# Background steps held behind a matmul, statistics moved into a later pass: one change to a Trainium2 kernel

## The chip, the cores and the metric

The kernel runs on one core of a Trainium2 chip. The core has a matrix engine (TensorE, PE in the profile; PEld is its weight load), VectorE (DVE), ScalarE (ACT), GpSimd (POOL) and SyncE (SP). In this kernel every DMA is issued from SP's queue. Each engine takes its instructions in the order written into the program and waits at the head of its queue until what that instruction needs is there. The metric is the device time in microseconds (us) of one execution.

## The reference

Two blocks work on one layer-normed input x of 2048 tokens by 1024 features, in float32.

```python
xn = layernorm(x)
q, k, v = heads(xn @ wqkv)                      # 32 heads of 32
phi(p) = concat(softmax(p @ w_phi), softmax(-(p @ w_phi)))
kv = sum over tokens of phi(k)^T v ;  z = sum over tokens of phi(k)
s = (phi(q) kv / (phi(q) z + 1e-6)) @ wo
h = sigmoid(xn @ w_gate) * (xn @ w_up)          # 3584 wide
g = silu(h @ w_down)
out = x + s * g
```

## The kernel before, in words

**Products.** Every large product is split twice. Each float32 operand becomes a high part (cast to the matrix engine's float32r on ACT, line 133) and a low part (a subtraction on DVE, line 134): the *split*. A product is then three matmuls (`mm3`, lines 142 to 144). On top of that each product of 2x2 blocks is done with seven block products instead of eight, named B11, B21, T2, T3, T4, T1, B22; their operands are block sums and differences, which POOL, DVE or, for chunk 0, the opening makes.

**Order.** The 2048 tokens are two chunks of 1024. After a hand-ordered opening (layer norm of chunk 0 and its V projection), the loop over `ops` runs: the rest of chunk 0's projections (K, then Q); pass 0 of the gate and up products (B11, B21 for 14 tiles); chunk 1's projections V, K, Q; pass 1 (T2, T3, T4 for 14 tiles); pass 2 (T1, B22). The down projection, the attention and the output follow, without the plan described next. An op is four quarter units of 12 matmuls, one for each of four banks; after each unit the bank is emptied (*evicted*) by ACT or DVE and written again by the next op.

**The plan of background steps.** All else is cut into steps that `later(n, f)` puts n quarter units ahead; `tick()`, called after each unit, traces those due. The steps that matter here:
- *x statistics* (`x_stats`, line 588): a 512 KB load of a token tile of chunk 1 into a slot of the ring `xstat`, then `x_moments` (two bn_stats and a bn_aggr on DVE, lines 595 and 596); `x_scales` makes scale and shift from all eight, `x_rows` turns them with 16 transposes on PE (line 607) into rows in slots 24 and 25.
- *x tasks* (`x_task`, line 611): load a transposed tile of chunk 1 (line 614) and two blocks of chunk 0 (line 617), apply the rows on DVE (line 625), make the block sums on POOL and store them.
- *q steps*: load a block of Q, spread it (lines 462 to 466), exponentials (line 470), sums and reciprocals, store. *k steps* (`k_load`, `k_spread`, `k_rest`, `kv_products`): the same for K, then a product of phi(k) with V on PE (line 520), into banks 4 to 7. ACT copies V and phi(k) (lines 507 and 508) for it.
- *weight sums* of the gate and up weights (`glu_sums`, line 376: four loads, `w_sums` with four POOL instructions, lines 280 to 283, and stores), *wo sums* (`o_sums`), and *operand loads* (`fetch_operand`, line 246: two loads at line 252, into slots 43 and 44, each with a split two or three units later).

**Who may stand where.** A planner orders each engine's queue at compile time with a timing of its own. What is traced earlier has precedence, but what is ready earlier may go first. `tc.issue_after(ins)` keeps instructions that are traced inside it, and that run on the engine of `ins`, from going ahead of `ins` in that queue; it adds no wait. In `tick()` (line 155) that `ins` is `last_dve[0]`, the last split or eviction of DVE traced so far. `queue2` does the same on SP behind the last weight load or projection store.

**Evictions and seeds.** `proj_out` (line 418) empties a projection's bank: copies on ACT, adds on DVE (line 432), and a store to `qkv_d` (line 425). In pass 1 each bank starts a tile from a seed: `fetch` (line 1099) loads four blocks of partial sums (line 1105), `seed` (copy at line 1115) puts them into the banks on ACT after the tile before is evicted.

Of the kernel before, what the change touches and what calls it, by code (L numbers as in the profile page):

```python
# [10 lines left out]
F32 = mybir.dt.float32  # L11
# [13 lines left out]
CTT = CT // P  # L25
# [20 lines left out]
B11, T2, T3, B21, T1, T4, B22 = range(7)  # L46
# [3 lines left out]
def hedgehog_glu_kernel(  # L50
# [12 lines left out]
    nc = tc.nc  # L63
# [29 lines left out]
    def block(name, first, n, dtype):  # L93
        again = blocks.get(name, (None, 0))[1]
        t = sb.tile([P, n, 2, HB], dtype, name=f"{name}_{again}", tag=name, bufs=1)
        blocks[name] = t, again + 1
        for i in range(n):
            slots[first + i] = t[:, i]
            where[first + i] = name, i
        return t  # L100
# [19 lines left out]
    def halves(*ids):  # L120
        return [slots[i][:, a] for i in ids for a in range(2)]
# [13 lines left out]
        last_dve[:] = [i.ins]  # L135
        return i

    last_dve = []

    def mm3(o, a, b, first, last, **kw):  # L140

        nc.tensor.matmul(o, a[0], b[0], start=first, stop=False, **kw)  # L142
        nc.tensor.matmul(o, a[0], b[1], start=False, stop=False, **kw)  # L143
        nc.tensor.matmul(o, a[1], b[0], start=False, stop=last, **kw)  # L144

    def cut(ab, s):
        return ab[0][:, s], ab[1][:, s]
# [4 lines left out]
    def later(n, f, *a):  # L152
        plan.setdefault(clock[0] + n, []).append((f, a))

    def tick():

        clock[0] += 1
        for f, a in plan.pop(clock[0], []):
            with tc.issue_after(last_dve[0]):
                f(*a)  # L160

    side = deque()
# [420 lines left out]

    ln8 = sb.tile([P, 4, CTT], F32, name="ln8")
    ws8, mv8 = ln8[:, :3], ln8[:, 2:]
    xstat = Ring((50, 51))

    def x_stats(n):
        xt = x_load(CTT + n, xstat.next())
        later(2, x_moments, n, xt)  # L590

    def x_moments(n, xt):
        st = small.tile([P, 2, 2, 6], F32, name=f"bn{CTT + n}", tag="bn")
# [498 lines left out]
    def queue2(n, f, *a):  # L1092

        def go():
            with tc.issue_after(last_load[0]):
                f(*a)
        later(n, go)
# [68 lines left out]
    sums = deque((f, s) for f in range(NJ) for s in range(2))  # L1166

    def begin_projection(c):

        if c == 0:  # L1170
            for k in range(4):
                queue2(4 * (4 + 2 * k), o_sums, k, halves(52, 53))
            for n in range(CTT):
                later(8 + 4 * n, x_stats, n)
            later(44, x_scales)
            return
        for t in range(EARLY):
            k_steps(1 + 9 * t, 0, t)
        for n in range(WEARLY):
            queue2(14 + 42 * n // WEARLY, glu_sums, *sums.popleft(), halves(43, 44))  # L1180

    def begin_pass(p):

        if p == 0:
            for n, k in enumerate(4 * a + q for q in range(4) for a in range(2)):
                later(4 + 8 * n, x_task, k)
            for n in range(NJ):
                q_steps(4 + 7 * n, n // 2, n % 2)
        elif p == 1:
            at = 1  # L1190
            for t in range(EARLY, 2 * TT):
                k_steps(at, *divmod(t, TT))
                at += 6
                if t % TT == TT - 1:
                    k_end(at + 2, t // TT)
                    at += 14
            for n in range(len(sums)):
                queue2(3 + 6 * n, glu_sums, *sums.popleft(), halves(43, 44))
        else:
            for n in range(NJ):  # L1200
                queue2(6 + 7 * n, wd_sums, n, halves(43, 44))
            qf_raw.items, qf_e.items = halves(52), (53, 54)
            for n in range(2):
                q_steps(8 + 40 * n, 7, n)

    phase = 0
    for n, (kind, c, what, i) in enumerate(ops):
# [3 lines left out]
        if kind == "proj":  # L1211
            if n == 8 or (c and (what, i) == (PROJ[0], B11)):
                begin_projection(c)
            first_slot = (XO1 if c else XO)[i]
            xo = run(first_slot, 4)
            for u in range(4):
                if i in opening:
                    pbank[u] = pmm.next()
                us = slice(u * P, (u + 1) * P)
                for k in range(4):  # L1220
                    mm3(pbank[u], (xo[:, k, 0, us], xo[:, k, 1, us]), pair(ws[k]),
                        i in opening and k == 0, k == 3, skip_group_check=True)
                step()
                proj_out(c, what, i, u, pbank[u])
                if c and (what, i) == (Q, B22):
                    seed(0, u)
                if u < 3:
                    tick()
            flow["used"] += 4
            while prep():  # L1230
                pass
            if what == Q:
                if c == 0:
                    if i == T2:
                        load_outer(B11, 1)
                    if i == T4:
                        block("x6", 24, 4, F32)
                        for q in range(4):
                            later(1 + q, x_rows, q)
                if c:  # L1240
                    m = order.index(i)
                    if m < 6:
                        load_outer((T2, T2, T3, T3, T4, T4)[m], m % 2)
                    if i == T1:
                        phase = 1
                        fetch(0)
                    if i == B22:
                        block("x1", 4, 4, F32)
                        m1 = halves(4, 5, 6, 7)
            tick()  # L1250
            continue

        phase, f = c, what
        m = f * len(PASSES[phase]) + PASSES[phase].index(i)
        if m == 0:
            if phase == 0:
                step(1000)
                for b in (0, 2):
                    block(f"x{b}", 4 * b, 4, F32)
            begin_pass(phase)  # L1260
        if (phase, i) in ((1, T3), (2, T1)):
            fetch(f + 1)
        for b in range(4):
            s, th = divmod(b, 2)
# [25 lines left out]
                pass  # L1290

        if phase == 0:
            for o in {18: (B11,), 19: (B21,), 20: (T2,), 26: (T3, T4), 27: (T1, B22)}.get(m, ()):
                load_operand(XO1[o], xo_d[o])
            if m == 27:
                block("p", 36, 2, F32R)
                block("p2", 38, 1, F32R)
        elif phase == 1 and (f, i) == (NJ - 2, T4):
            load_outer(T1, 0)
        elif phase == 1 and f == NJ - 1:  # L1300
            if i == T2:
                load_outer(T1, 1)
                load_outer(B22, 0)
            elif i == T3:
                load_outer(B22, 1)
            else:
                for b in (3, 5):
                    block(f"x{b}", 4 * b, 4, F32)
                uvfree.extend(halves(45, 46, 47, 50, 12, 13, 14, 15, 20, 21, 22, 23))
                hs_r.items = halves(48, 49, 51)  # L1310
                phase = 2
                fetched.clear()
                fetch(0)
        elif phase == 2 and f == NJ - 2 and i == T1:
            wfree.extend(range(16, 20))
# [266 lines left out]
```

## Time and profile before

| | |
|---|---|
| median of 3 runs | 2398.32 us (2398.09 to 2399.51) |
| the profiled execution | 2396.47 us |
| its span, first to last instruction | 2394.7 us |
| PE busy | 2364.6 us |
| DVE / ACT / POOL busy | 1605.9 / 1052.3 / 960.7 us |
| DMA queue of SP | 658 MB, 78.5% of 16 DMA engines' time |
| granted TensorE clock | 0.997 |

The profile comes from one execution. Its rows name an engine, the line of the code, the operation and the tiles (out<-in, buffer numbers left out); in a timeline row the two first numbers are the start and the length in us, and a bracket at the end tells how long the engine stood idle before it and what released it. A row "A <- B: total, times, longest" is a wait of A for B. In the tables by stretch each engine has its busy time, with the number of its instructions in parentheses; then come the granted clock, the DMA engines' busy share and GB/s. Matmuls are pipelined, so their lengths overlap. The opening ends near 145 us, chunk 0's projections run to 281 us, pass 0 to 586, chunk 1's projections to 843, pass 1 to about 1310.

### The profile page before, as it was taken

What the parts mean: (1) busy time and instruction counts of PE and PEld (TensorE: products, weight loads), DVE (VectorE), ACT (ScalarE), POOL (GpSimd) and SP (SyncE); (2) the same over time, 40 slices, a digit from 0 to 9 for tenths busy, and PEclk for the clock granted to TensorE, in tenths of its full rate; (3) what the DMA queues carried; (4) which work ended last, traced back from release to release, by engine and by line L of the source; (5) the groups of instructions that cost most, each with busy time, mean ns of one, the idle gap of its engine ahead of it and who ended that gap; (6) DMA issues with size and microseconds to landing.
All of it is one profiled execution on the core that took longest, in us unless ns stands there. A gap on an engine that the chain in (4) does not pass through costs nothing.

```text
span 2394.7 us, 32086 instructions
## 1 busy us (share of the span) xinstructions
PE 2364.6 (99%) x10972; PEld 1969.3 (82%) x10972; DVE 1605.9 (67%) x2103; ACT 1052.3 (44%) x1601; POOL 960.7 (40%) x617
## 2 busy tenths in 40 slices
PE   9999999999999899999999999999999999999999
PEld 8887888888888678788888888888888888888887
DVE  8636755653787677676655544344889988877776
ACT  7333444454433356555556322223443334455553
POOL 1233144621245125553001387785333334423556
PEclk9999999999999999999999999999999999999999
DMA  8799998884788899998554999897666766876665
GB/s 292 266 306 363 367 326 315 318 297 156 257 308 308 281 329 327 341 334 293 178 193 167 356 357 362 314 326 287 221 211 230 240 216 215 281 271 234 199 205 182
DMA packets 293492, 660.29 MB, mean 276 GB/s; under 512 B 37328, under 2 KB 37584, under 8 KB 288720
## 3 DMA queue, kind: packets, MB, share of 16 engines
q1 hardware_dynamic: 293328, 658.24, 78.5%
q8 instruction: 86, 1.41, 0.2%
q14 instruction: 78, 0.64, 0.1%
HBM read 393.61 MB, written 264.50 MB: 275 GB/s over the span
## 4 chain that ended last, share of the span: by engine, by line
PE 84%; DMA 7%; DVE 3%; POOL 3%; ACT 1%; issue 1%; SPq 1%; POOLq 0%; DVEq 0%; ACTq 0%
PE bank L142 26%; PE bank L143 26%; PE bank L144 26%; DMA fb<-w_gu 2%; PE bank L790 1%; PE bank L766 1%; DMA wg_d<-fb 1%; PE bank L331 1%; DMA qkv_d<-fc 1%; PE bank L520 1%; POOL fb L281 1%; DMA fc<-wo 1%; POOL fb L280 1%; DVE w L134 1%; DMA fb<-xr_d 1%
## 5 line engine op out<-in xcount | busy, mean ns | idle before, releaser
L142 PE MATMUL bank<-x,w 128*128 128x512 f32 x2352 | 916.0, 390 | 4.7 <-ACT bank L1115 4.0
L143 PE MATMUL bank<-x,w 128*128 128x512 f32 x2352 | 916.1, 390 | 0.0
L144 PE MATMUL bank<-x,w 128*128 128x512 f32 x2352 | 915.0, 390 | 0.0
L134 DVE TENSOR_TENSOR w<-fa,w 128x512 fp32r<-128x512 f32 (+1 forms) x458 | 431.6, 947 | 384.3 <-ACT w L133 380.7
L133 ACT CAST w<-fa 128x512 fp32r<-128x512 f32 (+1 forms) x458 | 310.7, 682 | 540.5 <-PE bank L143 408.5
L142 PEld LDWEIGHTS bank<-x,w 128*128 128x128 f32 x2352 | 442.1, 188 | 97.1 <-ACT bank L1115 4.4
L144 PEld LDWEIGHTS bank<-x,w 128*128 128x128 f32 x2352 | 441.9, 188 | 92.2 <-DVE w L134 0.4
L143 PEld LDWEIGHTS bank<-x,w 128*128 128x128 f32 x2352 | 442.0, 188 | 90.4
L142 PE MATMUL bank<-w,x 128*128 128x512 f32 x708 | 278.8, 394 | 15.4 <-DVE fc L432 15.3
L143 PE MATMUL bank<-w,x 128*128 128x512 f32 x708 | 276.8, 391 | 0.0
L144 PE MATMUL bank<-w,x 128*128 128x512 f32 x708 | 276.8, 391 | 0.0
L142 PEld LDWEIGHTS bank<-w,x 128*128 128x128 f32 x708 | 133.6, 189 | 43.6 <-DVE fc L432 14.6
L144 PEld LDWEIGHTS bank<-w,x 128*128 128x128 f32 x708 | 133.4, 188 | 28.0 <-DVE x L966 0.3
L280 POOL TENSOR_TENSOR fb<-fb 128x512 f32<-128x512 f32 x28 | 42.1, 1503 | 283.7 <-DMA fb<-w_gu 212.9
L143 PEld LDWEIGHTS bank<-w,x 128*128 128x128 f32 x708 | 133.6, 189 | 26.3
L722 POOL TENSOR_TENSOR fc<-fc 128x1024 f32<-128x1024 f32 x32 | 81.9, 2559 | 177.9 <-ACT fc L470 127.6
L1119 ACT COPY fc<-bank 128x512 f32<-128x512 f32 x168 | 97.5, 584 | 93.1 <-PE bank L144 55.0
L134 DVE TENSOR_TENSOR x<-fa,x 128x512 fp32r<-128x512 f32 x112 | 113.0, 1009 | 23.8 <-ACT x L133 23.8
L1157 DVE TENSOR_TENSOR x<-x,bank 128x512 f32<-128x512 f32 x72 | 49.4, 686 | 104.6 <-PE bank L144 102.4
L734 POOL TENSOR_TENSOR fc<-fc,sa 128x1024 f32<-128x1024 f32 x32 | 70.0, 2187 | 89.5 <-DVE sa L731 82.7
L133 ACT CAST x<-fa 128x512 fp32r<-128x512 f32 x112 | 69.2, 618 | 57.5 <-DMA fa<-wd_d 29.6
L432 DVE TENSOR_TENSOR fc<-fc,bank 128x512 f32<-128x512 f32 x84 | 56.3, 676 | 38.1 <-PE bank L144 25.0
(287 smaller groups left out, 3126.5 us busy)
## 6 DMA issues: line engine op xcount, KB each, us to landing
m_d<-fc SPq DMA_DIRECT2D x168, 256.0 KB, 4.7
fa<-h_d SPq DMA_DIRECT2D x84, 512.0 KB, 4.1
fa<-wf_d SPq DMA_DIRECT2D x32, 1024.0 KB, 6.9
x<-m_d SPq DMA_DIRECT2D x124, 256.0 KB, 5.1
h_d<-fc SPq DMA_DIRECT2D x114, 256.0 KB, 5.1
fb<-w_gu SPq DMA_DIRECT2D x112, 256.0 KB, 4.7
wg_d<-fb SPq DMA_DIRECT2D x112, 256.0 KB, 4.4
fa<-wg_d SPq DMA_DIRECT2D x56, 512.0 KB, 5.5
```

The source lines that it names most:

```text
L133: nc.scalar.copy(o[0], src)
L134: i = nc.vector.tensor_sub(o[1], src, o[0].bitcast(F32))
L142: nc.tensor.matmul(o, a[0], b[0], start=first, stop=False, **kw)
L143: nc.tensor.matmul(o, a[0], b[1], start=False, stop=False, **kw)
L144: nc.tensor.matmul(o, a[1], b[0], start=False, stop=last, **kw)
L280: nc.gpsimd.tensor_add(a22, a21, a22)
L281: nc.gpsimd.tensor_sub(a21, a11, a21)
L432: last_dve[:] = [nc.vector.tensor_add(y, x, b).ins]
L722: nc.gpsimd.tensor_mul(ez, e, zb)
L734: nc.gpsimd.tensor_mul(e3, e3, r2[:, :, None].to_broadcast([P, 32, DH]))
L1119: nc.scalar.copy(o, banks[b])
L1157: last_dve[:] = [nc.vector.tensor_add(us[b], us[b], banks[b]).ins]
```

## The change

- Inside `tick()`, steps are traced after `last_mm[0]`, the last matmul of the latest `mm3`, instead of `last_dve[0]`. So their PE instructions can't go ahead of that matmul in PE's queue; their DVE instructions are no longer held in DVE's.
- The eight x statistics and `x_scales` move from chunk 0's K and Q projections (units 8 to 36, and 44) to the start of pass 0 (units 1 to 4 and 7 to 10, scales at 15), the moments three units after the load instead of two. Their slots are 0 to 3 instead of 50 and 51. `x_rows` moves from Q's T4 to units 16 to 19 of pass 0, and with it the reuse of block x6 (slots 24 to 27).
- The x tasks start at unit 18 of pass 0 instead of 4 and are 7 units apart instead of 8. The loads of the first three operands for chunk 1 (B11, B21, T2) come one op later.
- In pass 1 the weight sums start at unit 8 instead of 3, and the seeds of the next tile are fetched at T2 instead of T3.

```diff
-    last_dve = []
+    last_dve, last_mm = [], []
...
-        nc.tensor.matmul(o, a[1], b[0], start=False, stop=last, **kw)
+        last_mm[:] = [nc.tensor.matmul(o, a[1], b[0], start=False, stop=last, **kw).ins]
...
         for f, a in plan.pop(clock[0], []):
-            with tc.issue_after(last_dve[0]):
+            with tc.issue_after(last_mm[0]):
                 f(*a)
...
-    xstat = Ring((50, 51))
+    xstat = Ring((0, 1, 2, 3))
 
     def x_stats(n):
         xt = x_load(CTT + n, xstat.next())
-        later(2, x_moments, n, xt)
+        later(3, x_moments, n, xt)
...
                 queue2(4 * (4 + 2 * k), o_sums, k, halves(52, 53))
-            for n in range(CTT):
-                later(8 + 4 * n, x_stats, n)
-            later(44, x_scales)
             return
...
         if p == 0:
+            for n in range(CTT):
+                later(1 + n + 2 * (n > 3), x_stats, n)
+            later(15, x_scales)
+            for q in range(4):
+                later(16 + q, x_rows, q)
             for n, k in enumerate(4 * a + q for q in range(4) for a in range(2)):
-                later(4 + 8 * n, x_task, k)
+                later(18 + 7 * n, x_task, k)
...
             for n in range(len(sums)):
-                queue2(3 + 6 * n, glu_sums, *sums.popleft(), halves(43, 44))
+                queue2(8 + 6 * n, glu_sums, *sums.popleft(), halves(43, 44))
...
-                    if i == T4:
-                        block("x6", 24, 4, F32)
-                        for q in range(4):
-                            later(1 + q, x_rows, q)
...
-                for b in (0, 2):
+                for b in (0, 2, 6):
                     block(f"x{b}", 4 * b, 4, F32)
             begin_pass(phase)
-        if (phase, i) in ((1, T3), (2, T1)):
+        if (phase, i) in ((1, T2), (2, T1)):
             fetch(f + 1)
...
-            for o in {18: (B11,), 19: (B21,), 20: (T2,), 26: (T3, T4), 27: (T1, B22)}.get(m, ()):
+            for o in {19: (B11,), 20: (B21,), 21: (T2,), 26: (T3, T4), 27: (T1, B22)}.get(m, ()):
                 load_operand(XO1[o], xo_d[o])
```

## The prediction

> **What bounds the kernel now.** I read the page first: its span and busy shares.
>
> ```profile
> span 2394.7 us, 32086 instructions
> ...
> PE 2364.6 (99%) x10972; PEld 1969.3 (82%) x10972; DVE 1605.9 (67%) x2103; ACT 1052.3 (44%) x1601; POOL 960.7 (40%) x617
> ```
>
> TensorE (PE) is busy for all but 30.1 us of the span, and the change neither adds nor removes a matmul. It can only win what PE waits for, or add to it. So the second view is the list of PE's waits. It has eleven rows; the first two carry nearly all of it, the third shown is a small one:
>
> ```profile
> PE bank L142 <- DVE fc L432: 15.3, 3, 11.4
> PE bank L142 <- ACT bank L1115: 4.0, 1, 4.0
> ...
> PE bank L520 <- DVE p L514: 0.9, 1, 0.9
> ```
>
> The first two are four stalls. The timeline of PE gives three of their places, in three short windows (the fourth, the small rest of 15.3, is at 236 us):
>
> ```profile
> 194.91 0.50 PE L142 MATMUL bank<-w,x 128*128 128x512 f32 x1 [2.22 <-DVE fc L432]
> 810.79 0.80 PE L142 MATMUL bank<-w,x 128*128 128x512 f32 x1 [11.38 <-DVE fc L432]
> 847.84 0.50 PE L142 MATMUL bank<-x,w 128*128 128x512 f32 x1 [3.98 <-ACT bank L1115]
> ```
>
> I call them A (194.9, 2.2 us), B (236, 15.3 - 2.2 - 11.4 = 1.7 us), C (810.8, 11.4 us) and D (847.8, 4.0 us). The third table, by stretch, adds a price that the wait rows don't show: after C and D the granted clock is low for some microseconds.
>
> ```profile
> core 0: us, PE busy (x) PEld busy (x) DVE busy (x) ACT busy (x) POOL busy (x), PEclk, DMA share, GB/s
> 812.00:815.00 3.00, 3.00 (x9) 2.33 (x8) 3.00 (x4) 2.16 (x3) 0.00 (x0) 0.53 0.58 188
> 849.00:852.00 3.00, 3.00 (x9) 2.31 (x8) 3.00 (x6) 2.34 (x4) 0.00 (x0) 0.50 1.02 365
> 281.00:311.00 30.00, 30.00 (x134) 24.86 (x133) 13.11 (x21) 12.89 (x22) 3.22 (x3) 1.00 1.04 411
> 815.00:843.00 28.00, 28.00 (x128) 23.32 (x128) 25.70 (x33) 12.38 (x15) 0.00 (x0) 1.00 0.82 276
> 624.00:799.00 175.00, 174.99 (x794) 145.51 (x793) 138.26 (x141) 55.97 (x65) 80.06 (x48) 1.00 0.85 298
> ```
>
> At full clock 134 matmuls start in 30 us, 0.224 us each, or 13.4 in 3 us; after the stalls only 9 do. That is 4.4 x 0.224 = 1.0 us lost in each of these rows, and the PE rows at half speed reach about as far again on either side: I take 2 us for C and 2 us for D. So C is worth 13.4, D 6.0, A and B 3.9: 23.3 us in all, 1.0% of the time. One quarter unit, the step that the plan counts in, is 12 matmuls: 2.7 us.
>
> **Part 1: chunk 1's statistics leave the first chunk's projections.** Stall A in the timeline of VectorE (DVE):
>
> ```profile
> 188.93 0.69 DVE L432 TENSOR_TENSOR fc<-fc,bank 128x512 f32<-128x512 f32 x1 [9.20 <-DMA qkv_d<-fc]
> 189.53 1.22 DVE L134 TENSOR_TENSOR w<-fa,w 128x1024 fp32r<-128x1024 f32 x1
> 190.67 2.46 DVE L595 BATCH_NORM_STATS2 bn<-fc 128x6 f32<-128x512 f32 x4
> 193.05 1.21 DVE L134 TENSOR_TENSOR w<-fa,w 128x1024 fp32r<-128x1024 f32 x1
> 194.17 0.68 DVE L432 TENSOR_TENSOR fc<-fc,bank 128x512 f32<-128x512 f32 x1
> ```
>
> PE at 194.91 starts as the eviction of 194.17 ends. Four statistics instructions, 2.46 us, stand ahead of it; without them it ends at 192.4 and the 2.2 us are gone. The loads go too (the stretch, and its DMA issues):
>
> ```profile
> 176.00:240.00 64.00, 60.09 (x264) 48.98 (x263) 39.46 (x50) 22.70 (x32) 21.34 (x14) 1.00 0.95 349
> ```
>
> ```profile
> fc<-x SPq DMA_DIRECT2D x6, 512.0 KB, 5.5
> ```
>
> Six of the eight loads lie in these 64 us, 3 MB at 349 GB/s = 9 us of a DMA that is 95% busy (the 9.20 us wait above is for a store that landed late). That helps B, which stands behind transfers of wo: I take half of its 1.7. Part 1 here: -2.2 - 0.8 = **-3.0** (bounds -3.9 and 0).
>
> What it adds at the start of pass 0: eight loads on SP's queue, 16 statistics of 0.68 us = 10.8 us and small ones on DVE, spread over 13 quarter units = 35 us. From 281 to 311 us alone DVE has 30 - 13 = 17 us free. DMA hasn't (1.04), but the x tasks' loads that fill it now start 14 units later. The 16 transposes of the scales, which end one place behind the last projection today, are only due 16 units (43 us) into the pass; the statistics need two rounds of four slots, each some 6 us to land plus four times 1.4 us on DVE: 23 us. Cover gone would mean PE waiting in its own queue for the scales, some 5 us. I take 0.
>
> The x tasks start later (18 for 4) and are planned closer (7 units for 8). Their buffers pace them, not the plan:
>
> ```profile
> L625 DVE TENSOR_TENSOR fc<-fc,x x16: 1208/1218/1935, 317.4 to 465.2; 128x1024 f32<-128x1024 f32 x16
> ```
>
> Eight tasks, two instructions each, in pairs: three intervals of a pair in 148 us are 49 us, over the 16 units (43 us) planned. In the new plan the first can't run before unit 20 (281 + 54 = 335 us), and three intervals later it is 482, 17 us later than today. The first operand made from them is loaded at op 19 (unit 79, 494 us) and used at 586 us; the other loads come behind it, the last at op 27 as before. Cost 0; the cover is those 90 us.
>
> **Part 2: what the steps are queued behind.** Today a step's DVE instructions may not stand ahead of the last split or eviction traced before it; PE, ScalarE (ACT), GpSimd (POOL) and SP are free, and the planner puts them where its own timing has them ready. Afterwards only the steps' PE instructions (k products, transposes, scale rows, broadcasts) are held, behind the unit's last matmul, and DVE is free too. No instruction is added. Two effects, of opposite sign.
>
> For the k chain it is good. Its PE products are now the held point, and load, spread, exponentials and sums of the next tile can be done ahead of it, as far as the single buffers let them. Today the sums wait for late data on ACT, and that is part of C (rows of ACT, of DVE, of SP):
>
> ```profile
> 789.17 0.62 ACT L507 CAST p<-fc 128x512 fp32r<-128x512 f32 x1 [12.44 <-DMA fc<-qkv_d]
> ...
> 804.23 1.04 ACT L133 CAST x<-fb 128x1024 fp32r<-128x1024 f32 x1 [11.59 <-DMA fb<-xr_d]
> ```
>
> ```profile
> 797.33 1.43 DVE L509 TENSOR_TENSOR p<-fc,p 128x512 fp32r<-128x512 f32 x1
> 807.57 2.36 DVE L134 TENSOR_TENSOR x<-fb,x 128x1024 fp32r<-128x1024 f32 x2 [8.82 <-ACT x L133]
> 809.85 0.35 DVE L476 RECIPROCAL stk<-stk 128x32 f32<-128x32 f32 x1
> 810.11 1.22 DVE L432 TENSOR_TENSOR fc<-fc,bank 128x512 f32<-128x512 f32 x2
> ```
>
> ```profile
> 792.38 6.17 SPq L380 DMA_DIRECT2D wg_d<-fb  x4
> ...
> 799.13 1.70 SPq L252 DMA_DIRECT2D fb<-xr_d  x2
> ```
>
> Read C from below: SP stores the last weight sum at 792 to 798 and only then loads the outer operand, whose buffers (43, 44) are the sum's; ACT waits for it until 804, DVE's split for ACT, and the eviction that PE needs stands behind the split until 810. The 12.4 us wait for the V load before it goes with the chain loaded ahead. The second wait stays: the twelve sums of this phase set it, not DVE's order. The last row of the table by stretch is theirs, from the first sum's loads to the operand's: 48 POOL instructions, twelve sums of four, 80 us of POOL's work in 175 us, the rest waits for loads: 14.6 us a sum, against the 42/12 units = 9.5 us planned. The change leaves these sums alone. What can move is the split's place in DVE's queue: with a chain that is less late, one eviction more may stand ahead of it, one quarter unit. C: **-2.7**, nearer to the "stays" end (0) than to all of it (-13.4), because the last wait is for a DMA that comes after the sums. The end above zero is a split that stands two units earlier (its step is due two units after the load; without the hold it follows ACT's cast directly): +5.4.
>
> D hangs on PE's own past. The chain of waits there:
>
> ```profile
> 833.04 5.98 DMA qkv_d<-fc
> 839.03 6.93 DMA fc<-m_d
> ...
> 846.26 1.04 ACT p L508
> ```
>
> The seeds use the last projections' store buffers: store, load (13 us together), a k cast in front on ACT, then the seed at 847.2. From 815 to 843 DVE is busy 25.7 of 28 us (table by stretch) with k steps and splits in a heap; the k steps of that heap (sums 6 us, spread 3 us by the rows of the chain) go forward, and the 1.04 us cast too, so the evictions ahead of the store come earlier. D: **-1.5** of 6.0 (bounds -6.0 and 0, or +2 where the loads land as late as 8 us).
>
> The bad effect is on steps that hang on a DMA alone: q steps and x tasks in pass 0, operand splits. Held, they came two units (5.4 us) after their load; free, they stand where the planner thinks the load lands, and a late one stops DVE's queue, evictions and weight splits behind it. How long the x tasks' loads (line 614) take today:
>
> ```profile
> DMA to landing us min/median/max: 6.4/6.8/8.0
> ```
>
> A wait of 2 or 3 us is covered: a bank is written again three units (8.2 us) after it is full, and in pass 0 DVE empties only two of eight banks per tile, ACT the rest. Weights are split four ops ahead. One wait of C's size would cost 13.4. Between 0 and that I take **+0.5**, as the third row of PE's waits, 0.9 us, is what one of today's small lags of DVE costs, and I expect half of one. The 14 q steps, no longer held, will also run together early in pass 0 (a load of 256 KB, stores of 512 KB by their tiles); DMA is at 1.04 from 281 to 311 us, so it will throttle them, and weights come four ops ahead. 0.
>
> **Part 3: small moves.** The seeds' loads one op (11 us) earlier in pass 1: four SP issues pass that op's weight load, which is wanted four ops later; no wait for seeds is in the list after D. 0. Weight sums five units (13.5 us) later in pass 1: 4 loads, 4 POOL sums and 4 stores each leave the crowded 843 to 857 us; the first is wanted at unit 72, prefetched from 56, so 45 units are left. 0, a part of D's gain at most.
>
> **Sum.** -3.0 - 2.7 - 1.5 + 0.5 = -6.7 us. The profiled execution took 2396.5 (span 2394.7 and 1.8 around it), 1.8 under the median of the runs, 2398.3; its stalls are taken as those of the median run. 2398.3 - 6.7 = **2391.6 us**, 0.28% faster.
>
> **Rivals.** (1) *Only part 1 counts.* C and D are made by sums and stores that the change doesn't touch; the order around them stays. -3.0: 2395.3, no difference (0.2%, 4.8 us, is what a measurement of this kernel can tell). For it: the SP rows. (2) *C goes.* If the planner's order puts the two evictions ahead of the operand's split, as the lighter queue allows, PE never stops there: -3.9 - 13.4 - 3 = 2378. For it: the 12.4 us V wait is half of why DVE was behind. Against: 14.6 us a sum. (3) *Slower: a freed DVE step stops the queue.* Place: the outer operands' twelve loads (799 to 849 us) or the opening of chunk 1. The split stands two units earlier and waits for the same load: C grows by 5.4; one more such wait on one of the next loads costs up to 13.4. 2398.3 - 3.0 + 5.4 = 2400.7 to 2398.3 - 3.0 + 5.4 + 13.4 = 2414; the middle is 2407. It decides from a DVE wait for a DMA of over 8 us in front of an eviction. For it: ACT, which is not held today, waits 11.6 us at the head of its queue. Against: from 281 to 311 and from 624 to 799 us (table by stretch) PE is busy 30.00 of 30 and 174.99 of 175 us, with DMA at 1.04 and 0.85 and ACT free. (4) *POOL slows.* The second of a sum's four instructions takes 1.29 to 2.16 us:
>
> ```profile
> L281 POOL TENSOR_TENSOR fb<-fb,fb x28: 1289/1621/2159, 631.8 to 1097.5; 128x512 f32<-128x512 f32 x28
> ```
>
> If the longer ones (2.16) are those beside DVE work, k steps pulled in front of 799 (two tiles of some 9 us in 175, 5% more overlap) add 48 x 0.05 x 0.87 = 2 us to the sums and to C: 2393.7, inside the range. The Trainium skill, "SBUF — State Buffer", section "SBUF: two separate sides", gives such a rule: VectorE instructions with two SBUF inputs and GpSimd lock each other out of one pair of ports for a whole instruction. The two lengths agree with it, and it speaks against freeing DVE; the size is small by the rows.
>
> **How the numbers follow.** My forecast (gains of A, some of B to D): 0.30. (1) 0.18; (2) 0.17; (3) 0.32; (4) 0.03, counted with no difference. Faster by over 0.2%: 0.30 + 0.17 = 0.47; within 0.2%: 0.21; slower: 0.32. The range goes from (2) to the middle of (3) and a little beyond, 2377 to 2411; all stalls gone would be 2375.
>
> **What would show it.** Right: no PE wait near 190 us; statistics (bn) between 281 and 320; scale rows at 325 without a PE wait; no ACT wait of 12 us for qkv_d before 800; C between 5 and 11 us and still behind an xr_d load; D under 4. Wrong: a PE wait at DVE in pass 0, a C over 13, or a new stall at 590 to 700. If C is gone, the error is my belief that the sums alone set it.

## The result and the profile after

The changed kernel takes **2405.76 us** (median of 19 executions), the kernel before, run beside it, 2395.96 us (19 executions): a ratio of **1.0039, 95% interval 1.0029 to 1.0049**. The change makes the kernel 0.4% slower. The forecast was 2391.6 us, a gain of 0.28%.

The profiled execution took 2404.75 us. The page of the changed kernel answers the one of before: PE is busy 4.1 us longer (matmuls at a low clock) and idle 4.2 us longer, 34.3 of the span.

```profile
span 2403.0 us, 32082 instructions
...
PE 2368.7 (99%) x10972; PEld 1969.6 (82%) x10972; DVE 1622.8 (68%) x2103; ACT 1043.8 (43%) x1593; POOL 958.3 (40%) x617
```

The list of waits, PE's rows first, then three of DVE's (engine, line, what it waited for: total us, times, longest):

```profile
PE bank L142 <- DVE fc L432: 10.8, 6, 2.8
PE bank L142 <- ACT bank L1115: 5.8, 4, 2.5
PE bank L142 <- DVE ln L596: 3.1, 1, 3.1
PE bank L142 <- DVE fb L1157: 2.6, 2, 1.9
PE bank L1040 <- POOL ident masks.py:199: 1.5, 1, 1.5
PE bank L142 <- ACT fb L1149: 1.4, 1, 1.4
...
DVE w L134 <- ACT w L133: 221.6, 93, 11.6
...
DVE stk L462 <- DMA fc<-qkv_d: 43.2, 14, 6.8
...
DVE fc L511 <- DMA zb_d<-fc: 8.2, 1, 8.2
```

The first row had three waits, one of them of 11.4 us; now it has six of at most 2.8 us. Rows 3 and 6 are new, and row 4 (line 1157) was 0.6 us before. The row to look at is the second one shown of DVE: the spread of K (line 462) waits 14 times, 43.2 us, for its load at the head of DVE's queue. The list of the kernel before has no such row; there DVE waited 380.7 us for casts of weights (line 134 for 133), now 221.6.

Because stalls split and low clocks follow them, I also worked out of each trace what PE lost: every gap between the starts of two matmuls over the usual gap for their shape, sums of those over 0.1 us. This holds the stall and the slow matmuls behind it. By stage, in us (145 to 240: chunk 0's projections; 240 to 300: their end and the opening of pass 0; 700 to 830 and 830 to 880: where C and D were; 880 to 1330: pass 1), with the ratio of the times:

| kernel | ratio to before [95%] | 145-240 | 240-300 | 300-590 | 700-830 | 830-880 | 880-1330 | 1330-2000 | rest | sum |
|---|---|---|---|---|---|---|---|---|---|---|
| before | 1 | 6.7 | 0.2 | 0.0 | 13.7 | 5.8 | 2.5 | 1.0 | 4.4 | 34.2 |
| e2_again: before, once more | | 6.0 | 0.2 | 0.0 | 12.3 | 6.7 | 4.1 | 1.1 | 5.3 | 35.8 |
| **after** | 1.0039 [1.0029, 1.0049] | 4.9 | 5.0 | 1.8 | 10.1 | 5.3 | 3.3 | 3.1 | 8.7 | 42.1 |
| e1_anchor: hold alone | 1.0006 [0.9995, 1.0016] | 5.9 | 0.0 | 0.0 | 13.5 | 1.5 | 3.8 | 3.2 | 8.2 | 36.1 |
| e1_stats: statistics alone | 1.0005 [0.9991, 1.0020] | 5.7 | 0.0 | 0.0 | 13.8 | 6.1 | 2.8 | 2.5 | 7.6 | 38.5 |
| e1_pass1: pass 1 alone | 1.0017 [1.0004, 1.0030] | 8.3 | 1.8 | 0.0 | 12.7 | 3.4 | 8.7 | 1.5 | 5.7 | 42.0 |
| e1_hold: after, both holds | 1.0017 [1.0003, 1.0030] | 5.4 | 0.0 | 0.0 | 8.7 | 4.0 | 6.7 | 1.3 | 7.8 | 33.9 |
| e4_anch_stats: after without pass 1 | 1.0026 [1.0013, 1.0039] | 3.5 | 5.5 | 1.7 | 12.9 | 4.2 | 3.6 | 3.6 | 6.7 | 41.7 |
| e4_anch_p1: after without statistics | 1.0013 [1.0000, 1.0025] | 4.1 | 0.0 | 0.0 | 16.7 | 4.5 | 6.2 | 6.6 | 6.7 | 44.9 |
| e2_ten: before, 10 early sums | 0.9978 [0.9968, 0.9989] | 7.0 | 0.2 | 0.0 | 8.6 | 0.0 | 5.6 | 1.6 | 8.6 | 31.8 |
| e3_eight: before, 8 early sums | 0.9967 [0.9956, 0.9979] | 4.7 | 0.2 | 0.0 | 1.4 | 0.0 | 9.9 | 1.5 | 6.9 | 24.6 |
| e4_after_eight: after, 8 early sums | 0.9996 [0.9986, 1.0007] | 5.5 | 4.9 | 1.7 | 0.0 | 0.0 | 10.6 | 5.5 | 7.4 | 35.6 |

From before to after the sum grows by 7.9 us and the span by 8.3: the table holds nearly the whole difference of these two executions. Two profiles of one program (rows 1 and 2) differ by up to 1.6 us in a stage, and the 19 executions of the kernel before spread by 0.45%. So a stage's number is evidence only where it is far from both rows of before, and sizes of whole edits are taken from the ratios.

**Where the time came from.** C (700 to 830) shrank by 2 to 4 us, D hardly, chunk 0's projections by 1 to 2; against that stand about 5 us at 270, 1.8 us in pass 0 and 2 us in pass 2. The last column, 4 us more, lies in the opening and the down projection; e2_ten, which changes nothing there, shows 8.6 as well, so I don't count it as an effect. So only 3.6 of the 7.9 us lie in the stages named here; the medians differ by 9.8 us. The 2 us of pass 2 belong to the free DVE: from 1330 to 2000 us the five kernels of the table without DVE's hold lose 3.1 to 6.6 us, the others 1.0 to 2.5. Four places show the mechanism. Timeline of DVE in the changed kernel (start, length, in brackets the idle time before it and what ended it):

```profile
267.64 1.21 DVE L134 TENSOR_TENSOR w<-fa,w 128x1024 fp32r<-128x1024 f32 x1
268.77 0.20 DVE L596 BATCH_NORM_AGGREGATE ln<-bn 128x2 f32<-128x12 f32 x1
268.89 2.19 DVE L134 TENSOR_TENSOR w<-fa,w 128x1024 fp32r<-128x1024 f32 x1
271.00 1.27 DVE L595 BATCH_NORM_STATS2 bn<-x 128x6 f32<-128x512 f32 x2
272.20 0.67 DVE L432 TENSOR_TENSOR fb<-fb,bank 128x512 f32<-128x512 f32 x1
...
717.43 0.69 DVE L462 TENSOR_REDUCE stk<-fc 128x16 f32<-128x512 f32 x1 [4.02 <-DMA fc<-qkv_d]
718.04 0.68 DVE L463 TENSOR_REDUCE stk<-fc 128x16 f32<-128x512 f32 x1
718.63 1.44 DVE L513 TENSOR_TENSOR fc<-fc 128x1024 f32<-128x1024 f32 x1
719.99 0.68 DVE L432 TENSOR_TENSOR fc<-fc,bank 128x512 f32<-128x512 f32 x1
...
798.10 0.69 DVE L462 TENSOR_REDUCE stk<-fc 128x16 f32<-128x512 f32 x1 [6.83 <-DMA fc<-qkv_d]
798.70 0.68 DVE L463 TENSOR_REDUCE stk<-fc 128x16 f32<-128x512 f32 x1
799.29 0.68 DVE L432 TENSOR_TENSOR fc<-fc,bank 128x512 f32<-128x512 f32 x1
...
1348.22 1.67 DVE L465 TENSOR_TENSOR fc<-fc,stq 128x512 f32<-128x512 f32 x1 [1.27 <-DMA zb_d<-fc]
1349.81 1.76 DVE L466 TENSOR_TENSOR fc<-stq,fc 128x512 f32<-128x512 f32 x1
1351.49 0.67 DVE L1157 TENSOR_TENSOR fb<-fb,bank 128x512 f32<-128x512 f32 x1
```

Each time a step's instructions stand in front of an eviction (lines 432, 1157), at 717, 798 and 1348 us after a wait for a DMA. The timeline of PE has the other end of each wait:

```profile
273.01 0.47 PE L142 MATMUL bank<-w,x 128*128 128x512 f32 x1 [3.14 <-DVE ln L596]
...
720.72 0.80 PE L142 MATMUL bank<-w,x 128*128 128x512 f32 x1 [2.81 <-DVE fc L432]
...
800.02 0.50 PE L142 MATMUL bank<-w,x 128*128 128x512 f32 x1 [1.07 <-DVE fc L432]
...
1352.22 0.50 PE L142 MATMUL bank<-x,w 128*128 128x512 f32 x1 [1.90 <-DVE fb L1157]
```

The profile puts the first of these waits down to the short statistic of 272.78 (line 596), which ends 0.1 us after the eviction of 272.20; weight splits (line 134) stand in that heap as well. The 1.8 us of pass 0 are of another kind: at 403.6 us PE waits 1.4 us for an eviction by ACT (line 1149), ahead of which an exponential of a q step (line 470) runs from 400.6 us. They come only in profiles with at least part of DVE's steps free and the statistics and x tasks moved.

The first place shows a second surprise: the statistics, planned for pass 0 (from 281 us), run from 261.6 to 291.1 us, so nine of the sixteen stand in the last projections, where evictions are due.

### The profile page after: what moved, and what is told of

Same layout as the page of the kernel before. It is cut to its first block, busy times and chain, and to the rows that moved or that the text cites. A ratio compares the mean times of both kernels' runs of the same rounds, so it can differ in the third digit from the quotient of the medians.

```text
span 2403.0 us, 32082 instructions
## 1 busy us (share of the span) xinstructions
PE 2368.7 (99%) x10972; PEld 1969.6 (82%) x10972; DVE 1622.8 (68%) x2103; ACT 1043.8 (43%) x1593; POOL 958.3 (40%) x617
## 4 chain that ended last, share of the span: by engine, by line
PE 74%; DMA 12%; DVE 7%; POOL 3%; issue 2%; ACT 1%; SPq 1%; DVEq 0%; POOLq 0%; ACTq 0%
PE bank L142 23%; PE bank L144 23%; PE bank L143 23%; DMA fb<-w_gu 3%; DVE w L134 2%; PE bank L790 1%; PE bank L766 1%; DMA qkv_d<-fc 1%; DMA fb<-xr_d 1%; DVE x L134 1%; DMA wg_d<-fb 1%; PE bank L331 1%; PE bank L520 1%; DMA fc<-wo 1%; DMA wf_d<-fc 1%
## 5 line engine op out<-in xcount | busy, mean ns | idle before, releaser
L134 DVE TENSOR_TENSOR w<-fa,w 128x512 fp32r<-128x512 f32 (+1 forms) x458 | 443.4, 974 | 234.7 <-ACT w L133 221.6
L432 DVE TENSOR_TENSOR fc<-fc,bank 128x512 f32<-128x512 f32 x84 | 56.3, 679 | 36.1 <-PE bank L144 31.7
```

Of the source, the lines that this page charges most:

```text
L134: i = nc.vector.tensor_sub(o[1], src, o[0].bitcast(F32))
L432: last_dve[:] = [nc.vector.tensor_add(y, x, b).ins]
```

## The experiments

Two theories were open after that. The first: freeing DVE is what costs, because steps that hang on a DMA, or are simply early, get ahead of evictions. The rival: the order on DVE hardly matters, and what costs is the work that was put elsewhere (statistics and x tasks into pass 0, weight sums later in pass 1). A third question stood beside them: what makes C, which the change was forecast to shrink.

### The parts one by one, and the change with DVE held as well

e1_anchor, the hold alone (`last_mm` kept by `mm3` as in the diff above):

```diff
-            with tc.issue_after(last_dve[0]):
+            with tc.issue_after(last_mm[0]):
```

> The kernel before with the hold alone changed: steps behind the last matmul instead of the last DVE instruction. Theory F (freed DVE steps stand ahead of evictions and wait there for their loads; the profile after has 14 waits of the k spread, line 462, for its load, 43 us in all, where before has none): most of the loss is here, ratio 1.002 to 1.006, with the waits of L462 for qkv_d and the big stall C (11.4 us) split into smaller ones. Theory M (the loss comes from the moved statistics and x tasks): within 0.2% of before, ratio 0.998 to 1.002.

e1_stats, the lines of the statistics, rows, x tasks and operand loads alone; e1_pass1, two lines alone:

```diff
-                queue2(3 + 6 * n, glu_sums, *sums.popleft(), halves(43, 44))
+                queue2(8 + 6 * n, glu_sums, *sums.popleft(), halves(43, 44))
...
-        if (phase, i) in ((1, T3), (2, T1)):
+        if (phase, i) in ((1, T2), (2, T1)):
```

> The kernel before with the statistics, scale rows, x tasks and first operand loads moved as in the change, the hold and pass 1 as before. My prediction's part 1 says -3.0 us (stall A gone, half of B), ratio 0.9985 to 1.000; theory F says the same. Theory M: slower, ratio 1.002 to 1.005, with the PE wait for the statistics (line 596, 3.1 us at 270 us in the profile after) still there.

> The kernel before with only pass 1 changed: seeds fetched one op earlier, weight sums five units later. Prediction: 0 us, ratio 0.999 to 1.001, stall D (4.0 us) 0 to 1.5 us shorter. If the loss sits here: over 1.002, with PE waits for seeds (line 1115) between 880 and 1310 us, where the profile after has 2.7 us and before none.

e1_hold, the whole change, but the steps held behind both:

```diff
-            with tc.issue_after(last_mm[0]):
+            with tc.issue_after(last_mm[0]), tc.issue_after(last_dve[0]):
```

> The changed kernel with its steps held behind both the last matmul (PE) and the last DVE instruction (DVE). Theory F: the waits of L462 for qkv_d go (under 5 us in all) and the time comes back to before or under it, ratio 0.996 to 1.001. Theory M: stays at 1.003 to 1.005. If holding the PE steps is what costs, it also stays above 1.002, without L462 waits.

Measured: 1.0006, 1.0005, 1.0017 and 1.0017 (intervals in the table). Neither theory has it alone. The hold by itself costs nothing that these runs can tell, though the waits that theory F named are there (41.3 us at line 462). Holding DVE again removes all of these waits and takes 1.0039 down to 1.0017, but not to the 1.001 or less that theory F gave; by the two intervals this gain is 0.05 to 0.39%. What remains is as much as the pass 1 part costs by itself. In e1_pass1 no PE wait for a seed came from 880 to 1330 us. Here the waits of DVE in e1_anchor, from 590 to 843 us, beside the same stretch of the kernel before:

```profile
DVE stk L462 <- DMA fc<-qkv_d: 17.7, 5, 6.9
DVE x L134 <- ACT x L133: 14.2, 8, 3.5
DVE w L134 <- ACT w L133: 12.9, 8, 6.3
```

```profile
DVE w L134 <- ACT w L133: 33.5, 14, 7.3
DVE x L134 <- ACT x L133: 11.1, 4, 8.8
```

The waits for K's loads come with the hold alone. In that kernel's profile D falls to 1.5 us beside them, though the others with DVE free and twelve early sums (4.2 to 5.3) don't repeat it. So a wait at the head of DVE's queue is not a loss by itself; it is one where an eviction behind it is due.

### Why later weight sums cost

A theory that the results left was a clash of two rhythms: sums from unit 8 on, every six units, might fall on the units of the k steps. e2_sums8 moves the sums as the change does and leaves the fetch of the seeds; e2_sums9 starts them one unit later; e2_again is the kernel before, profiled once more.

```diff
-                queue2(3 + 6 * n, glu_sums, *sums.popleft(), halves(43, 44))
+                queue2(9 + 6 * n, glu_sums, *sums.popleft(), halves(43, 44))
```

> The kernel before once more, unchanged, for one profile: how far PE's stalls differ between two executions of one program. If they are fixed by the order, each stage's loss comes again within 1 us (145 to 240 us: 6.7, 700 to 830: 13.7, 830 to 880: 5.8, 880 to 1330: 2.5, after 1330: 2.8). If DMA timing sets them, stages differ by several us and only effects beyond that can be read from one profile.

> The kernel before with only the weight sums of pass 1 five units later (8 + 6n for 3 + 6n). Theory P (a sum's POOL instructions now stand ahead of the mask's memset in the k end at units 45 to 57, and PE's transposes, line 555, wait for it at the head of PE's queue): the L555 wait for POOL fb L282 of 2 to 4 us is there, and the ratio is that of the whole pass 1 part, 1.001 to 1.003. Theory Q (the earlier seeds' loads cost): ratio 0.999 to 1.001, no such wait.

> The same with 9 + 6n: six units later, so each sum stands where the next one stood, and the k end meets the sums as before. Theory P: no L555 wait over 1 us, ratio 0.999 to 1.001. If delaying the sums is itself the cost: as with 8, 1.001 to 1.003.

Measured: 1.0016 [1.0006, 1.0027] and 1.0019 [1.0006, 1.0032]. So the sums alone make the cost of this part, the seeds' earlier fetch adds nothing that shows, and the clash of phase falls, since one unit more changes neither the time nor PE's wait at line 555 (2.8 us in e2_sums9). The waits of PE in pass 1 of e2_sums8, and its timelines of ACT and of POOL there:

```profile
PE bank L520 <- DVE p L514: 2.6, 1, 2.6
PE bank L555 <- POOL fb L282: 2.3, 1, 2.3
```

```profile
1097.48 0.62 ACT L507 CAST p<-fc 128x512 fp32r<-128x512 f32 x1 [5.26 <-DMA fc<-qkv_d]
...
1104.75 1.05 ACT L508 CAST p<-fc 128x1024 fp32r<-128x1024 f32 x1 [4.66 <-DVE fc L504]
```

```profile
1098.86 1.29 POOL L280 TENSOR_TENSOR fb<-fb 128x512 f32<-128x512 f32 x1 [7.07 <-DMA fb<-w_gu]
1100.23 1.62 POOL L281 TENSOR_TENSOR fb<-fb,fb 128x512 f32<-128x512 f32 x1
```

The later sums still run at 1099 us, where the last k products (line 520) are due. In the kernel before the two rows of PE are 0.9 (line 520) and 0.6 us (line 555). Line 555 are the transposes at the end of the k chain; ahead of them stands a memset (line 547) on POOL's queue, and POOL waits for a sum's load. In e2_again the wait of line 555 is 2.5 us as well, without any edit, but there PE waits for another POOL instruction (line 1135), and the wait at line 520 does not appear. With later or more sums in pass 1 and DVE held, it is the sum's line 282 in every profile: 2.3 to 4.0 us in eight kernels. So sums that stand in the way at the end of the k chain are seen each time; the wait at line 520 runs from none to 5.6 us in the same eight, and how the 0.16% divides is not settled.

### What makes C

e2_ten and e3_eight change one number of the kernel before, how many weight sums are done early, in chunk 1's projections (`WEARLY`); the others follow in pass 1. e3_tenhold is e2_ten with the steps held behind both. e4_six goes on to six.

```diff
-    EARLY, WEARLY = 9, 12
+    EARLY, WEARLY = 9, 10
```

> The kernel before with ten instead of twelve weight sums in chunk 1's projections (the other two go to pass 1). My step on stall C says the twelve sums, 14.6 us each, set when the outer operand is loaded: two fewer free its buffers some 29 us earlier, C (11.4 us and 2 us of low clock) goes, ratio 0.994 to 0.997. If the k chain or SP's queue sets C instead, it stays over 5 us and the ratio is 0.998 to 1.001.

> The kernel before with eight instead of twelve weight sums in chunk 1's projections (ten gave 0.9978, with a stall of 5.7 us left before the operand loads and one of 3.8 us in pass 1, line 555). If the sums' number alone sets the end of that phase: 0.994 to 0.997, no stall over 2 us from 700 to 880 us. If the sums that go to pass 1 cost there what they save here (as the later sums of the change did): 0.998 to 1.001, with more loss from 880 to 1330 us than with ten.

> The kernel before with ten sums, and the steps held behind both the last matmul and the last DVE instruction; nothing else of the change. If holding PE's steps is free and the ten sums carry the gain: 0.996 to 0.999, as with ten alone (0.9978). If holding PE's steps helps, since data are ready when PE gets there: under 0.9965 and no PE wait at line 520 over 1 us. If it costs: 0.999 to 1.002.

> The kernel before with six early sums for twelve. The theory that the sums ahead of the first outer operand made C is served already by ten and eight (0.9978, 0.9967): C stays gone, and each two sums moved behind it cost in pass 1, where the loss rose from 2.5 to 5.6 and 9.9 us. If that rise goes on: 14 us from 880 to 1330 us and a ratio of 0.998 to 0.999. If it was a coincidence of one place: 0.9960 to 0.9970.

Measured: 0.9978 [0.9968, 0.9989], 0.9967 [0.9956, 0.9979], 0.9977 [0.9969, 0.9986] and 0.9970 [0.9959, 0.9981]. SP's queue (first two issues of the first outer operand) in e2_ten, and the table by stretch of e3_eight:

```profile
770.80 0.32 SPq L252 DMA_DIRECT2D fb<-xr_d  x1
...
772.93 0.32 SPq L252 DMA_DIRECT2D fb<-xr_d  x1
```

```profile
core 0: us, PE busy (x) PEld busy (x) DVE busy (x) ACT busy (x) POOL busy (x), PEclk, DMA share, GB/s
700.00:830.00 130.00, 128.85 (x584) 106.81 (x583) 111.50 (x124) 54.04 (x62) 27.74 (x16) 1.00 0.84 286
830.00:880.00 50.00, 50.00 (x233) 41.87 (x232) 35.80 (x39) 25.33 (x39) 22.27 (x13) 1.00 1.00 366
880.00:1330.00 450.00, 442.74 (x2029) 368.57 (x2029) 289.26 (x339) 246.57 (x384) 153.96 (x97) 1.00 0.81 275
```

Two sums less bring the operand's load from 799 to 771 us, 28 us, near two sums of 14.6 us each. The next steps are smaller: with eight and six that load comes at 762 and 751 us. With ten, the 11.4 us wait for the split is gone, D with it, and one stall of 5.7 us at an ACT eviction is left, and the ratio missed the 0.994 to 0.997 expected; with eight, PE is busy 128.85 of 130 and 50.00 of 50 us. That C hangs on the sums ahead of the operand's load, as the prediction read it, is shown; whether through the buffers that both use or through their place in SP's queue, these runs don't separate. What is taken out there comes back in part in pass 1, whose loss rises from 2.5 to 5.6, 9.9 and 13.5 us with ten, eight and six, at the same two lines of PE (555 and 520) as in e2_sums8. With six, that loss is the 14 us of one theory and the ratio that of the other. **The kernel before with eight early sums, 2387.56 us, has the best ratio of all that ran**; that of six lies within its interval. Holding the steps behind both (e3_tenhold) does nothing to ten.

### Which freed step costs

e3_khold holds `k_spread` and `k_rest` of the changed kernel also behind `last_dve`, e3_xhold in their place `x_moments` and `x_scales` (these two kernels are three lines longer: their line 465 is 462 above, and so on).

```diff
-            with tc.issue_after(last_mm[0]):
-                f(*a)
+            with ExitStack() as es:
+                es.enter_context(tc.issue_after(last_mm[0]))
+                if f in (k_spread, k_rest):
+                    es.enter_context(tc.issue_after(last_dve[0]))
+                f(*a)
```

> The changed kernel with the k steps' DVE instructions (k_spread, k_rest) held behind the last DVE instruction again, all else of the change as it is. Theory K (the freed k spread, 43 us of waits for K loads at the head of DVE's queue, is the larger part of what freeing DVE costs, which is 1.0039 - 1.0017 = 0.22%): those waits go (under 5 us) and the ratio to before falls to 1.002 to 1.003. Theory X (the freed statistics cost it, 5 us lost from 240 to 300 us): stays 1.0035 to 1.005, the loss at 240 to 300 us stays.

> The changed kernel with only the statistics' DVE instructions (x_moments, x_scales) held again. Theory X: the loss from 240 to 300 us goes from 5.0 to under 1 us and the ratio falls by 0.2%, to 1.0015 to 1.0025. Theory K: the stage clears too, but the ratio stays 1.003 to 1.0045 because the L462 waits remain (some 40 us).

Measured: 1.0032 [1.0020, 1.0044] and 1.0031 [1.0019, 1.0043]; both lie within the interval of the whole change. Waits of e3_khold:

```profile
PE bank L142 <- DVE fc L435: 12.9, 3, 10.1
...
ACT p L510 <- DMA fc<-qkv_d: 40.6, 7, 11.7
```

With the k steps held, DVE's 43.2 us at K's loads are gone, ACT waits 40.6 us for V's, and C is back in one piece of 10.1 us: the wait was moved, not removed. With the statistics held, the loss from 240 to 300 us falls from 5.0 to 0.1, but C's stage shows 14.5 us and 300 to 590 3.3. K's waits stay there (55.1 us), and no gain in time shows; with the k steps held, the ratio fits neither theory (1.0035 or more, or 1.002 to 1.003), while the loss from 240 to 300 us stays at 4.4. Holding one kind of step did not bring the time of e1_hold, as far as five executions of each can tell.

### Do the parts add up?

The three parts alone sum to 0.28%, the change costs 0.39%. Two pairs of parts, and the change with the lighter sums:

> The hold and the pass 1 part, without the statistics. If the parts add up: 1.0006 + 0.0017, a ratio of 1.0023. If the rest of the cost is an interaction of the hold with pass 1: 1.0033 to 1.0039. If it is one of the hold with the statistics (the stall at 270 us), this kernel has no loss from 240 to 300 us and lies at or under 1.0023.

> The hold and the statistics, without the pass 1 part. If the parts add up: 1.0011. If the freed statistics are what costs (VectorE ahead of an eviction at 270 us, some 4 to 5 us with the low clock): a loss of 4 to 5 us from 240 to 300 us and a ratio of 1.002 to 1.003.

> The changed kernel with eight early sums. If C's cause acts there as before, the gain is the same, 0.33%: 1.0039 x 0.9967 = 1.0006. If the freed VectorE steps are what stops the queue from 700 to 830 us, whatever the sums: a ratio of 1.002 to 1.004, with stalls of 2.5 to 3 us left there. If the changed order serves a lighter queue better: under 0.9967.

e4_anch_p1 is the change without the lines of e1_stats, e4_anch_stats without those of e1_pass1, e4_after_eight the whole change with `WEARLY` at 8. Measured: 1.0013, 1.0026 and 0.9996. The statistics cost only when DVE is free. The rows of line 595 (x16: shortest, middle, longest in ns; first and last start) of e1_stats, then of e4_anch_stats:

```profile
L595 DVE BATCH_NORM_STATS2 bn<-x x16: 639/676/691, 298.7 to 326.0; 128x6 f32<-128x512 f32 x16
```

```profile
L595 DVE BATCH_NORM_STATS2 bn<-x x16: 644/680/697, 260.3 to 289.3; 128x6 f32<-128x512 f32 x16
```

The same steps at the same units run 38 us earlier when nothing holds them on DVE. The loads aren't held on SP in either kernel (they are issued from 254 to 256 us on, when slots 0 to 3, which hold T3's operand before, have come free), so the first data is there. The loss from 240 to 300 us is 5.0, 5.5 and 4.9 us in the three kernels that have the free DVE and the early statistics (after, e4_anch_stats, e4_after_eight), 4.4 in e3_khold, and 0.0 to 0.2 where one of the two is missing or the moments are held, but for 1.8 in e1_pass1, which are the slow matmuls behind a wait of 2.1 us that ends at 239.5. That stall is an interaction of parts 1 and 2, and this is shown. That it makes the whole 0.15% by which the pair exceeds its parts (1.0026 against 1.0006 + 0.0005) is not: with intervals of 0.0013 each, sum and pair can't be told apart by the times alone.

e4_after_eight, from 700 to 830 and from 830 to 880 us, has PE busy throughout, while DVE still waits for K's loads (its wait from 700 to 880 us; 12.4 us, 4 times, in the changed kernel):

```profile
700.00:830.00 130.00, 130.00 (x594) 108.38 (x593) 109.24 (x124) 55.68 (x64) 25.65 (x16) 1.00 0.86 289
830.00:880.00 50.00, 50.00 (x230) 41.70 (x229) 30.50 (x39) 27.03 (x41) 15.78 (x11) 1.00 0.96 346
```

```profile
DVE stk L462 <- DMA fc<-qkv_d: 8.9, 5, 5.2
```

So the rival of that expectation (freed steps stop the queue there, whatever the sums) falls: C in the changed kernel has the cause it had, the sums; the freed waits only cut it into pieces. The gain is 1.0039 to 0.9996, as large as before the change within the intervals, and 0.29% behind e3_eight remain, the price of the change elsewhere.

## Why the prediction was wrong

The range (2377 to 2411) held 2405.8, and so did the third rival (2400.7 to 2414). The forecast itself had the wrong sign. Its sum was -3.0 - 2.7 - 1.5 + 0.5. None of the signs that it gave for being wrong came: PE's wait in pass 0 is for ACT and not for DVE, C is not over 13, and from 590 to 700 us nothing is lost.

**The step that failed is the last term of part 2, the bad effect of freeing DVE, taken at +0.5 us.** It was costed as half of one small lag, because "a wait of 2 or 3 us is covered". The runs show 14 waits for K's loads, up to 6.8 us, one of 8.2 for a store of z, and statistics that are merely early. The evictions behind them came 1.1 to 3.1 us too late for PE in the rows shown: with the low clock behind the first, 5 us at 270, then 2.1 more than before around 1350, and the pieces of C. Held again (e1_hold), 0.22% go, 5 us: about ten times the term. Without the moved statistics the same freeing (e1_anchor) came to +1.4 us (-1.2 to +3.8), where part 2 as a whole was forecast at -3.7.

**"For the k chain it is good" was wrong in the same way.** Loading ahead "as far as the single buffers let" moved the 12.4 us wait from ACT's queue, where PE was busy 174.99 of 175 us in spite of it, to DVE's, where evictions wait behind it. The sign "no ACT wait of 12 us for qkv_d before 800" came true, and meant a DVE wait at 798. For C, -2.7 was near (10.1 for 12.3 to 13.7 us), but by luck: it counted on one eviction more ahead of the long wait for the split, while C fell into four waits of 1.1 to 2.8 us, two of them behind K's loads. In the other kernels with DVE free and twelve early sums the stage lost 12.9 to 16.7. What it said of C's cause is confirmed by ten and eight sums. For D, -1.5 can't be told from nothing in the change (5.3 for 5.8 and 6.7).

**Part 1, -3.0, is not seen.** The statistics alone give 1.0005 [0.9991, 1.0020], which is -2 to +5 us. A (194.9 us) and B are gone, as forecast; the 0.8 us wait at 190.7 is another one, which e1_anchor and e3_eight have too. But a new one stands behind them, where three splits precede an eviction:

```profile
209.78 0.47 PE L142 MATMUL bank<-w,x 128*128 128x512 f32 x1 [2.42 <-DVE fc L432]
```

It comes, at 2.1 to 2.4 us, in all seven profiles with the statistics moved and in none of the others, so it takes back much of the 3.9 us of A and B. In the changed kernel the place failed as well: planned for 281 to 320 us, the statistics ran from 261, since with DVE free they wait for their loads, and these for slots, and not for the plan. Scale rows without a PE wait at 334.7 to 344.6 and x tasks from 337.6 to 492.9 (estimated 335 and 482) were right.

**Part 3, 0, measured +0.17%, 4 us.** "45 units are left" looked at when the sums are wanted, not at what they now run beside: the last k steps of pass 1. That was measured on the kernel before; in the changed kernel's own profile pass 1 loses 3.3 us, no more than before (2.5 and 4.1).

**The rivals.** (3) came in by its time and by its mechanism, "a freed DVE step stops the queue". Its places, the outer operands' loads and the opening of chunk 1, and with them its sum, were wrong: from 700 to 880 us less is lost than before (15.4 for 19.5 us), and the new losses stand at 270, in pass 0 and at 1350. That the time fits is partly luck. Its sign, a DVE wait of over 8 us for a DMA ahead of an eviction, came once, in pass 1. Behind it stand on DVE two instructions of the k spread and an eviction (line 1151), on ACT an exponential and a seed (timelines of DVE, then of ACT):

```profile
1031.66 0.69 DVE L511 COPY fc<-fc 128x1024 f32<-128x1024 f32 x1 [8.16 <-DMA zb_d<-fc]
```

```profile
1033.71 1.06 ACT L470 ACTIVATE fc<-fc 128x1024 f32<-128x1024 f32 x1 [7.17 <-DVE fc L466]
1034.67 0.58 ACT L1115 COPY bank<-x 128x512 f32<-128x512 f32 x1
```

PE waits 2.3 us for that seed, until 1035.3; the forecast had set up to 13.4 us for such a wait. (4), POOL slowing, is not borne out. Line 281 in the changed kernel:

```profile
L281 POOL TENSOR_TENSOR fb<-fb,fb x28: 1275/1304/2272, 630.3 to 1127.0; 128x512 f32<-128x512 f32 x28
```

Its middle is 1304 ns for 1621 before, and from 624 to 796 us the 48 POOL instructions take 79.74 us for 80.06. The Trainium skill's rule ("SBUF — State Buffer", section "SBUF: two separate sides") may make the two lengths, about 1.3 us and up to 2.2 or 2.3, that both kernels have; no run here separates that, and no loss at POOL shows.

**What stays open**: how the 0.39% divides between the interaction and the parts, whose differences lie within the intervals; how much of the price of later sums is the k products' and how much the memset's; and where the changed kernel pays it, as its pass 1 shows none.

## What to carry to other kernels

A fence that keeps background work behind the last eviction is a cover: before taking it off, list what each freed instruction waits for, and count every DMA wait that can now stand at the head of the queue that empties banks. A step moved in the plan also moves to wherever its loads allow it, if only one engine holds it. When a stall ends at a load behind a heap of other work, as C did, change the size of the heap: one number, 12 to 8, gave 0.33%, more than any reordering here.

## What was unexpected in the hardware

After a stall of 2 or 3 us the clock may be low for some microseconds, or not. From 273 to 277 us in the changed kernel 11 matmuls ran in 3.99 us at a granted clock of 0.57, where 0.224 us each would make 18. So the wait of 3.1 us before them cost some 5, as the table shows; the forecast counted this for C and D, but not for new stalls. In the same profile slow matmuls follow the waits of 2.8 us (720.7) and 2.5 us (853.8) as well, and none those of 2.4 us (209.8) and 2.3 us (1035.3). Even one place differs between executions: in the eleven profiles that have stall A, of 2.2 to 2.3 us, matmuls at half speed (0.427 us apart) follow it in five, with a granted clock of 0.79 to 0.81 from 194 to 202 us, and in six none do, at 1.00. In e1_pass1 and e2_sums9 the clock is 1.00 even after waits of 3.1 us (849 us).

```profile
273.00:277.00 4.00, 3.99 (x11) 3.15 (x12) 0.53 (x1) 1.24 (x2) 1.29 (x1) 0.57 1.06 423
```

The 19 executions of the kernel before ran from 2390.83 to 2401.57 us on the same inputs. No single profile can show an effect of 0.2% by its span: e1_hold's profiled execution took 2395.78 us, while the median of its 12 timed ones was 2400.88.
